# Two small attentions feeding a max-out feed-forward: weights taken in column quarters, batch 0 run along with them, x^T and A^T by transposing DMAs

## The chip, the cores and the metric

The kernel runs on one core of a Trainium2 chip. The metric is device time in microseconds, median of several runs; lower is better. TensorE multiplies matrices and transposes (by a matmul with an identity), VectorE and ScalarE empty its PSUM banks and do elementwise work, GpSimd (POOL) does elementwise work on SBUF, and DMA queues issued from SyncE (SP), ScalarE and POOL move data. Each engine executes its own instructions in program order.

## The reference

B = 8 batches, H = 8 heads, S = 512 rows of x, 32 rows of state, D = 64:

```python
scores = scale * x @ state^T;  a = softmax(scores);  xread = a @ state        # [B,H,512,64]
scores2 = scale * state @ x^T; a2 = softmax(scores2); sread = a2 @ x          # [B,H,32,64]
attn = concat([xread, sread], axis=2)            # heads side by side: [8*544, 512]
out = maximum(attn @ w1, attn @ w2) @ w_out      # w1, w2: 512 x 1024, w_out: 1024 x 512
```

Inputs and output are float32; the kernel multiplies in bfloat16.

## The kernel before, in words

max(x w1, x w2) is computed as x w2 + relu(x (w1 - w2)). So `wcat` holds w1 - w2 (1024 columns) and beside it w2 @ w_out (512 columns), and for every batch the kernel multiplies the state by `wcat` once (`u_sw`, result `SW`, 1536 columns). With A^T, the transposed attention weights (`AT`), a batch's feed-forward (`moe`) is then: L1, 8 tiles of 2 matmuls SW^T A^T, each followed by a relu into `r`; L2, for 4 row blocks 2 matmuls of A^T with SW's last 512 columns and 8 of r with w_out; copy out and store.

The attention of a batch is a list of eight units (`att_units`): `u_xt` twice (8 TensorE transposes of x each and a copy out of PSUM), `u_sc` twice (8 small score matmuls, exp on ScalarE, row sums and reciprocal on VectorE, the normalising multiply on POOL), `u_sr` twice (the state rows' attention; a column of ones in xb gives its sums), `u_at` (8 transposes for A^T and a copy), `u_srt` (4 transposes of the state rows' result). The units of batches 0 to 2 run before the loop; those of batch b + 3 are put between the tiles of batch b's feed-forward, as is `u_sw` of batch b + 1. The order of instructions is the order of the program text.

Ahead of the loop: x of batches 0 to 2 and the states are loaded, then w2 and w1, each as two DMAs to 64 partitions, and w_out with a casting DMA from POOL's queue. `w_t` casts w2 and transposes it on TensorE (32 transposes), `w_wo` multiplies w2 by w_out (32 matmuls of 512 columns), VectorE subtracts w2 from w1, and `u_sw` runs for batch 0. `moe_sread` treats the state rows of all batches in one pass near the end. All PSUM tiles come from one pool of eight banks.

Copies, casts and exits from PSUM go through the helper `copy`, whose lines the profile shows: L58 is ScalarE, L60 VectorE, L62 POOL. L235 is L1, L244 and L246 are L2, L226 and L228 the relus, L147 the x transposes, L189 A^T, L197 the state rows' transposes, L178 `u_sr`, L213 `u_sw`, L161 the scores, L284 and L290 w2's transposes and its product.

Of the kernel before, what the change touches and what calls it, by code (L numbers as in the profile page):

```python
# [8 lines left out]
F32 = mybir.dt.float32  # L9
# [6 lines left out]
def kernel(  # L16
# [9 lines left out]

# [48 lines left out]
    load_x(0)  # L79
    s_f = stage.tile([128, B // 4, DM], F32)  # L80
    for b in range(B):
        nc.scalar.dma_start(
            out=s_f[32 * (b % 4):32 * (b % 4) + 32, b // 4, :].rearrange("n (h d) -> n h d", h=H),
            in_=state[b].rearrange("h n d -> n h d"),
        )
    load_x(1)
    load_x(2)
    w2f = stage.tile([128, 4, FF], F32)
    w1f = stage.tile([128, 4, FF], F32)
    for wf, w in ((w2f, moe_w2), (w1f, moe_w1)):  # L90
# [6 lines left out]
    wo = consts.tile([128, NF, DM], BF16)
    wcat = consts.tile([128, 4, WC], BF16)
    w2b = stage.tile([128, 4, FF], BF16)
    w2t = stage.tile([128, 4, NF, 128], BF16)  # L100


    s_bf = stage.tile([128, B // 4, DM], BF16)
    s_b2 = stage.tile([128, B // 4, 4, 2, D], BF16)
    sbd = consts.tile([128, B, 4, 2 * Ns], BF16)
    nc.vector.memset(sbd, 0.0)
    st2 = consts.tile([128, 4, B * Ns], BF16)

    def states(bb):
        copy("V", s_bf[:, bb, :], s_f[:, bb, :])  # L110
        p = bank(BF16)
        for k in range(4):
            nc.tensor.transpose(p[:, k * 128:(k + 1) * 128], s_bf[:, bb, k * 128:(k + 1) * 128], ident)  # L113
        for jj in range(2):
            copy("A" if jj else "V",
                 sbd[64 * jj:64 * jj + 64, 4 * bb:4 * bb + 4, :, 32 * jj:32 * jj + 32],
                 p[64 * jj:64 * jj + 64, 0:512].rearrange("p (k b n) -> p b k n", k=4, b=4))
        copy("P", s_b2[:, bb], s_f[:, bb, :].rearrange("p (g i d) -> p i g d", g=2, i=4))
        p = bank(BF16)
        for i in range(4):  # L120
            nc.tensor.transpose(p[:, i * 128:(i + 1) * 128], s_b2[:, bb, i].rearrange("p g d -> p (g d)"), ident)
        copy("V", st2[:, :, 128 * bb:128 * bb + 128],
             p[:, 0:512].rearrange("p (i t) -> p i t", i=4))


    sread_t = consts.tile([128, 4, B * Ns], BF16)
    AT, SW = {}, {}
    st = {}

    def cast_x(b, engs=("P", "P")):  # L130
        xb = xio.tile([128, NC, 2, 258], BF16, tag="xb", name="xb")
        nc.gpsimd.memset(xb[:, :, :, 256:257], 1.0)
        for g in range(2):
            copy(engs[g],
                 xb[:, :, g, 0:256].rearrange("p c (i d) -> p i c d", i=4),
                 xf_t[b][:, 4 * g:4 * g + 4, :].rearrange("p i (c d) -> p i c d", c=NC))
        st[b] = dict(xb=xb)

    def u_xt(b, half):
        d = st[b]  # L140
        if half == 0:
            d["xt"] = at.tile([128, NC, 4, 128], BF16, tag="xt", name="xt")
        p = bank(BF16)
        for cc in range(2):
            c = 2 * half + cc
            for k in range(4):
                nc.tensor.transpose(p[:, (cc * 4 + k) * 128:(cc * 4 + k + 1) * 128],  # L147
                                    d["xb"][:, c, k // 2, (k % 2) * 128:(k % 2) * 128 + 128], ident)
        copy("A" if half else "V", d["xt"][:, 2 * half:2 * half + 2].rearrange("p c k t -> p (c k t)"), p)

    def u_sc(b, half):
        d = st[b]
        if half == 0:
            d["e"] = at.tile([128, NC, H, Ns], BF16, tag="e", name="e")
            d["es"] = at.tile([128, NC, H], F32, tag="es", name="es")
            d["er"] = at.tile([128, NC, H], F32, tag="er", name="er")
            d["a"] = at.tile([128, NC, H, Ns], BF16, tag="a", name="a")
        p = bank()
        for cc in range(2):
            for k in range(4):  # L160
                nc.tensor.matmul(p[:, cc * 256 + k * 64:cc * 256 + k * 64 + 64],  # L161
                                 d["xt"][:, 2 * half + cc, k, :], sbd[:, b, k, :],
                                 start=(cc == 0 and k == 0), stop=(cc == 1 and k == 3))
        sl = slice(2 * half, 2 * half + 2)
        nc.scalar.activation(out=d["e"][:, sl].rearrange("p c h n -> p (c h n)"), in_=p, func=ACTF.Exp, scale=scale)  # L165
        nc.vector.tensor_reduce(d["es"][:, sl], d["e"][:, sl], axis=mybir.AxisListType.X, op=ALU.add)  # L166
        nc.vector.reciprocal(d["er"][:, sl], d["es"][:, sl])  # L167
        nc.gpsimd.tensor_mul(d["a"][:, sl], d["e"][:, sl],  # L168
                             d["er"][:, sl].unsqueeze(3).to_broadcast([128, 2, H, Ns]))

    def u_sr(b, g):
        d = st[b]
        if g == 0:
            d["sr"] = at.tile([128, 4, 2, D], BF16, tag="sr", name="sr")
            d["rr"] = at.tile([128, 2], F32, tag="rr", name="rr")
        p = bank()
        for c in range(NC):
            nc.tensor.matmul(p[:, 0:257], d["e"][:, c, 4 * g:4 * g + 4, :].rearrange("p i n -> p (i n)"),  # L178
                             d["xb"][:, c, g, 0:257], start=(c == 0), stop=(c == NC - 1))
        nc.vector.reciprocal(d["rr"][:, g:g + 1], p[:, 256:257])  # L180
        nc.vector.tensor_scalar(d["sr"][:, :, g, :], p[:, 0:256].rearrange("p (i d) -> p i d", i=4), scalar1=d["rr"][:, g:g + 1], scalar2=None, op0=ALU.mult)

    def u_at(b):
        d = st[b]
        AT[b] = keep.tile([128, 2, NC * 128], BF16, tag="at", name="aT")
        p = bank(BF16)
        for g in range(2):
            for c in range(NC):
                nc.tensor.transpose(p[:, (g * NC + c) * 128:(g * NC + c + 1) * 128],  # L189
                                    d["a"][:, c, 4 * g:4 * g + 4, :].rearrange("p i n -> p (i n)"), ident)  # L190
        copy("V", AT[b].rearrange("p g t -> p (g t)"), p)

    def u_srt(b):
# [12 lines left out]

    def u_sw(b, ch):
        if ch == 0:
            SW[b] = big.tile([128, 2, WC], BF16, tag="sw", name="sw")
        pg = [bank(), bank()]  # L210
        for i in range(4):
            for g in range(2):
                nc.tensor.matmul(pg[g][32 * i:32 * i + 32, :],  # L213
                                 st2[64 * g:64 * g + 64, i, b * Ns:(b + 1) * Ns],
                                 wcat[64 * g:64 * g + 64, i, ch * 512:(ch + 1) * 512],
                                 start=True, stop=True)
        for g in range(2):
            copy("A" if g else "V", SW[b][:, g, ch * 512:(ch + 1) * 512], pg[g])

# [10 lines left out]
    def moe(b, fill):  # L230
        r = big.tile([128, NF, NC * 128], BF16, tag="r", name="r")
        for f in range(NF):
# [4 lines left out]
            for u in fill.get(f, ()):  # L237
                u()
# [122 lines left out]
```

The softmax here doesn't subtract the row's maximum and nothing guards it: scores larger than these inputs give would overflow.

## Time and profile before

| | |
|---|---|
| median of 3 runs | 203.4 us (202.53 to 203.79) |
| span of the profiled execution, first to last instruction | 200.5 us |
| TensorE busy | 160.0 us (80%) |
| VectorE, ScalarE, POOL busy | 92.3, 70.6, 34.3 us |
| first L1 matmul of batch 0 | 64.44 us after the span's start |
| moved by DMA | 25.35 MB |

The run times are taken without the profiler; the profiled execution has only its span, and what lies around it (launch and end) is the difference to the medians. TensorE's matmuls are pipelined: one of 512 columns is shown as 379 ns long, while its successor starts 216 ns after it, so durations of groups are read from one start to the next start.

### The profile page before, as it was taken

The numbers are of one execution on the slowest core, as the hardware profiler recorded it, in microseconds if no ns is written. First come the engines' busy times: TensorE is split into PE (matmuls) and PEld (weight loads), VectorE is DVE, ScalarE is ACT, GpSimd is POOL, SyncE is SP. The second block draws the span as 40 slices with busy tenths as digits, with TensorE's granted clock in tenths as the row PEclk, the third lists the DMA queues.
The fourth block names the chain that finished last, engine by engine and source line by source line (L and its number), as shares of the span: only waits on it lengthen the run. The fifth ranks groups of instructions, "written<-read, shape, count | busy, mean of one in ns | idle before, by whom it ended". The sixth has DMA issues, their size and how long they took to land.

```text
span 200.5 us, 2915 instructions
## 1 busy us (share of the span) xinstructions
PE 160.0 (80%) x1192; PEld 83.1 (41%) x1192; DVE 92.3 (46%) x171; ACT 70.6 (35%) x123; POOL 34.3 (17%) x47
## 2 busy tenths in 40 slices
PE   0020364386599989999999999999999999999991
PEld 0010343365344545544644554554454474344440
DVE  1120262136686775484476458448436322632610
ACT  0050143740425812552281182255234230722311
POOL 1010491004340070043016007004000000000000
PEclk9999995566999999999999999999999999999999
DMA  5999999999100000480191075040013042300522
GB/s 179 308 301 227 215 215 219 246 348 309 50 3 0 0 5 0 168 252 3 52 304 65 0 233 190 0 183 29 0 52 157 3 167 67 80 3 0 211 105 105
DMA packets 16557, 25.35 MB, mean 126 GB/s; under 512 B 2848, under 2 KB 14112, under 8 KB 15648
## 3 DMA queue, kind: packets, MB, share of 16 engines
q1 hardware_dynamic: 13328, 23.60, 38.7%
q0 software_dynamic: 1040, 1.05, 3.1%
q10 hardware_dynamic: 2176, 0.52, 1.3%
q8 instruction: 9, 0.15, 0.3%
q14 instruction: 4, 0.03, 0.0%
HBM read 17.30 MB, written 8.91 MB: 131 GB/s over the span
## 4 chain that ended last, share of the span: by engine, by line
PE 61%; DMA 10%; DVE 9%; ACT 9%; POOL 6%; issue 3%; ACTq 1%; DVEq 0%; POOLq 0%
PE ps L246 24%; DMA s_f<-in_state_dram 10%; PE ps L235 9%; PE ps L244 6%; DVE es L166 4%; PE ps L290 3%; PE ps L147 3%; DVE r L228 3%; PE ps L213 3%; POOL a L168 3%; PE ps L178 2%; PE ps L189 2%; ACT e L165 2%; PE ps L284 2%; ACT xt L58 2%
## 5 line engine op out<-in xcount | busy, mean ns | idle before, releaser
L246 PE MATMUL ps<-wo,r 128*128 128x512 bf16 x256 | 61.3, 379 | 1.4 <-DVE r L228 1.4
L246 PEld LDWEIGHTS <-r 128*128 128x128 bf16 x256 | 25.0, 98 | 33.5 <-DVE r L228 3.9
L235 PE MATMUL ps<-aT,sw 128*128 128x512 bf16 x128 | 33.4, 380 | 0.1
L58 ACT COPY ob<-ps 128x512 f32<-128x512 f32 x16 | 9.4, 586 | 67.5 <-PE ps L246 67.5
L168 POOL TENSOR_TENSOR a<-e,er 128x512 bf16<-128x512 bf16 x16 | 16.6, 1048 | 85.1 <-DVE er L167 71.6
L228 DVE TENSOR_SCALAR r<-ps 128x512 bf16<-128x512 f32 x32 | 21.4, 670 | 11.0 <-PE ps L235 10.9
L226 ACT ACTIVATE r<-ps 128x512 bf16<-128x512 f32 x32 | 19.4, 607 | 4.8 <-PE ps L235 4.8
L244 PE MATMUL ps<-sw,aT 128*128 128x512 bf16 x64 | 19.2, 381 | 0.0
L60 DVE COPY ob<-ps 128x512 f32<-128x512 f32 x16 | 11.0, 688 | 17.5 <-PE ps L246 16.1
L113 PE MATMUL ps<-ident,s_bf 128*128 128x128 bf16 x8 | 1.2, 306 | 22.0 <-DVE s_bf L60 22.0
L60 DVE CAST sw<-ps 128x512 bf16<-128x512 f32 x24 | 16.2, 680 | 5.2 <-PE ps L213 5.2
L166 DVE TENSOR_REDUCE es<-e 128x16 f32<-128x512 bf16 x16 | 10.7, 670 | 9.2 <-ACT e L165 9.2
L58 ACT CAST sw<-ps 128x512 bf16<-128x512 f32 x24 | 13.9, 591 | 2.2 <-PE ps L213 2.2
L235 PEld LDWEIGHTS <-sw 128*128 128x128 bf16 x128 | 10.5, 98 | 9.3 <-issue 1.6
L62 POOL CAST xb<-xf 128x1024 bf16<-128x1024 f32 x14 | 14.2, 1042 | 0.0
L147 PE MATMUL ps<-ident,xb 128*128 128x128 bf16 x128 | 11.7, 252 | 0.0
L147 PEld LDWEIGHTS <-xb 128*128 128x128 bf16 x128 | 10.5, 117 | 2.4
L60 DVE COPY xt<-ps 128x1024 bf16<-128x1024 bf16 x8 | 5.5, 692 | 10.9 <-PE ps L147 10.9
L178 PE MATMUL ps<-xb,e 128*128 128x257 bf16 x64 | 9.7, 274 | 0.9 <-ACT e L165 0.6
L58 ACT COPY xt<-ps 128x1024 bf16<-128x1024 bf16 x8 | 8.1, 1009 | 5.3 <-PE ps L147 4.0
L113 PEld LDWEIGHTS <-s_bf 128*128 128x128 bf16 x8 | 0.7, 130 | 22.3 <-DVE s_bf L60 22.3
L165 ACT ACTIVATE e<-ps 128x512 bf16<-128x512 f32 x16 | 9.8, 612 | 0.0
(53 smaller groups left out, 140.6 us busy)
## 6 DMA issues: line engine op xcount, KB each, us to landing
xf<-in_x_dram SPq DMA_DIRECT2D x20, 512.0 KB, 7.3
out_dram<-ob SPq DMA_DIRECT2D x7, 1024.0 KB, 4.3
w2f<-in_moe_w_dram SPq DMA_DIRECT2D x2, 1024.0 KB, 12.3
w1f<-in_moe_w_dram SPq DMA_DIRECT2D x2, 1024.0 KB, 20.3
wo<-in_moe_w_out_dram POOLq DMA_DIRECT2D x1, 1024.0 KB, 18.2
out_dram<-ob SPq DMA_DIRECT2D x2, 512.0 KB, 2.6
s_f<-in_state_dram ACTq DMA_DIRECT2D x8, 64.0 KB, 6.9
out_dram<-obs SPq DMA_DIRECT2D x8, 64.0 KB, 1.7
```

The lines of the kernel that those rows point to most:

```text
L58: nc.scalar.copy(o, i)
L60: nc.vector.tensor_copy(o, i)
L62: nc.gpsimd.tensor_copy(o, i)
L147: nc.tensor.transpose(p[:, (cc * 4 + k) * 128:(cc * 4 + k + 1) * 128], d["xb"][:, c, k // 2, (k % 2) * 128:(k % 2) * 128 + 128], ident)
L165: nc.scalar.activation(out=d["e"][:, sl].rearrange("p c h n -> p (c h n)"), in_=p, func=ACTF.Exp, scale=scale)
L166: nc.vector.tensor_reduce(d["es"][:, sl], d["e"][:, sl], axis=mybir.AxisListType.X, op=ALU.add)
L168: nc.gpsimd.tensor_mul(d["a"][:, sl], d["e"][:, sl], d["er"][:, sl].unsqueeze(3).to_broadcast([128, 2, H, Ns]))
L226: nc.scalar.activation(out=o, in_=p, func=ACTF.Relu)
L228: nc.vector.tensor_scalar(o, p, scalar1=0.0, scalar2=None, op0=ALU.max)
L235: nc.tensor.matmul(p, SW[b][:, g, f * 128:(f + 1) * 128], AT[b][:, g, :], start=(g == 0), stop=(g == 1))
L244: nc.tensor.matmul(p, AT[b][:, g, cs], SW[b][:, g, FF:WC], start=(g == 0), stop=False)
L246: nc.tensor.matmul(p, r[:, f, cs], wo[:, f, :], start=False, stop=(f == NF - 1))
```

## The change

Weights come in four column quarters of 256, each as three DMAs to 128 partitions (w2, w1, w_out in float32, cast on an engine). State loads take 2 KB rows, those of batch 0 first. Batch 0's attention, L1 and L2 are cut to fit the quarters: each quarter is cast, transposed, subtracted and multiplied by the state (`sw`), then two L1 tiles and their share of L2 run, L2 accumulating in four PSUM banks over all quarters (`l2_part`, `l2_open`). w2 @ w_out is done in two halves (`w_wo`). Batch 1's attention lies in between, with TensorE transposes. From batch 2 on, x^T and A^T are written by transposing DMAs on SP's queue (`xt_dma`, `at_dma`), and a batch's attention runs within the batch before it: scores and normalisation after its L1, `sw` and `sread_mm` between its L2 blocks. `sread_mm` uses outputs of 64 partitions and a column of ones apart. PSUM is split in two pools of four banks: `ps`, and `pa` for L2 and the earliest work. At the start some matmuls on zeros run (`idle`). Cut to its core:

```diff
-    for wf, w in ((w2f, moe_w2), (w1f, moe_w1)):
-        for g in range(2):
-            nc.sync.dma_start(
-                out=wf[64 * g:64 * g + 64],
-                in_=w[256 * g:256 * g + 256].rearrange("(i d) f -> d i f", i=4),
-            )
+    def load_wq(q):
+        for wf, w, tag in ((w2f, moe_w2, "w2f"), (w1f, moe_w1, "w1f")):
+            wf[q] = stage.tile([128, 4, FQ], F32, tag=tag, bufs=3, name=tag)
+            nc.sync.dma_start(out=wf[q], in_=w[:, q * FQ:(q + 1) * FQ].rearrange("(i p) f -> p i f", p=128))
+        wof[q] = stage.tile([128, 2, DM], F32, tag="wof", bufs=3, name="wof")
+        nc.sync.dma_start(out=wof[q], in_=moe_w_out[q * FQ:(q + 1) * FQ, :].rearrange("(f p) n -> p f n", p=128))
...
+    def xt_dma(b):
+        d = st[b]
+        d["xt"] = at.tile([128, NC, 4, 128], BF16, tag="xt", name="xt")
+        nc.sync.dma_start_transpose(out=d["xt"].rearrange("p c k t -> p (c k) t"),
+                                    in_=d["xb"].rearrange("p c m -> p (c m)"))
...
+    def at_dma(b):
+        d = st[b]
+        AT[b] = keep.tile([128, 2, NC, 128], BF16, tag="at", name="aT")
+        nc.sync.dma_start_transpose(out=AT[b].rearrange("p g c t -> p (g c) t"),
+                                    in_=d["a"].rearrange("p g c i n -> p (g c i n)"))
...
+    def sread_mm(b, pool=None):
+        d = st[b]
+        p = bank(F32, pool)
+        d["srp"] = p
+        for c in range(NC):
+            xv = d["xb"][:, c].rearrange("p (i g d) -> p g i d", g=2, d=D)
+            for g in range(2):
+                for ih in range(2):
+                    nc.tensor.matmul(p[64 * ih:64 * ih + 64, g * 128:(g + 1) * 128],
+                                     d["e"][:, g, c, 2 * ih:2 * ih + 2].rearrange("p i n -> p (i n)"),
+                                     xv[:, g, 2 * ih:2 * ih + 2],
+                                     start=(c == 0 and g == 0), stop=(c == NC - 1 and g == 1), skip_group_check=True)
+        for g in range(2):
+            for c in range(NC):
+                nc.tensor.matmul(p[:, 256 + g:257 + g], d["e"][:, g, c].rearrange("p i n -> p (i n)"), ones[:, 0:1],
+                                 start=False, stop=(c == NC - 1), skip_group_check=True)
...
+    def l2_part(q, first):
+        for c in range(NC):
+            if first:
+                ACC[c] = bank(F32, pa)
+            l2_f(0, c, ACC[c], (2 * q, 2 * q + 1), first, False)
...
+    load_states(sf0, 0, 1)
+    load_x(0)
+    for q in range(3):
+        load_wq(q)
+    load_states(sfr, 1, B)
+    load_x(1)
+    load_wq(3)
+    load_x(2)
+    load_x(3)
...
+    idle(7)
+    states(sf0, sb0, 0, 1, "V", "A", "V", pa)
+    cast_x(0, ("V", "V"))
+    xt_pe(0, 0, "A", pa)
+    xt_pe(0, 1, "V", pa)
+    w2_cast(0, "P")
+    scores(0, 0)
+    w2_tr(0, "A")
+    norm(0, 0, "V")
+    scores(0, 1)
+    w_sub(0, 2, 4, "P")
+    norm(0, 1, "V")
+    w_sub(0, 0, 2, "V")
+    at_pe(0, ("A", "V"), pa)
+    wo_cast(0, "P")
+    sw(0, 0, FQ)
+    sread_mm(0, pa)
+    w2_cast(1, "A")
+    l1(0, 0)
+    l1(0, 1)
...
+    w_sub(1, 0, 2, "V")
+    w_sub(1, 2, 4, "P")
+    wo_cast(1, "P")
+    w2_tr(1, "V")
+    sw(0, FQ, 2 * FQ)
+    l2_part(0, True)
+    l1(0, 2)
+    l1(0, 3)
+    w2_cast(2, "A")
+    for i in range(4):
+        w_wo(0, i)
...
+    sread_tr(0, "A")
+    l2_part(1, False)
+    w2_tr(2, "V")
+    sw(0, 2 * FQ, 3 * FQ)
+    states(sfr, sbr, 1, B, "P", "A", "V")
+    cast_x(1, ("V", "A"))
+    l1(0, 4)
+    l1(0, 5)
+    xt_pe(1, 0, "A")
+    xt_pe(1, 1, "V")
+    w2_cast(3, "A")
+    l2_part(2, False)
+    scores(1, 0)
+    scores(1, 1)
+    w_sub(3, 0, 2, "V")
+    w_sub(3, 2, 4, "P")
+    norm(1, 0, "P")
+    norm(1, 1, "P")
+    wo_cast(3, "A")
+    w2_tr(3, "V")
+    sw(0, 3 * FQ, 4 * FQ)
+    l1(0, 6)
+    l1(0, 7)
+    cast_x(2, ("P", "P"))
+    xt_dma(2)
+    sread_mm(1)
+    for i in range(4):
+        w_wo(1, i)
+    sread_norm(1)
+    at_pe(1, ("A", "V"))
+    l2_part(3, False)
+    sw(1, 0, 512)
+    sw(0, FF, WC)
+    sw(1, 512, 1024)
+    for c in range(NC):
+        l2_open(0, c, ACC[c], False, True)
+        l2_out(0, c, ACC[c], "A" if c % 2 else "V")
...
+    for b in range(1, B):
+        n = b + 1
+        if b + 2 < B:
+            cast_x(b + 2, ("P", "P"))
+            xt_dma(b + 2)
         for f in range(NF):
...
+            l1(b, f)
         if n < B:
...
+            for hh in range(2):
+                scores(n, hh)
+            for hh in range(2):
+                norm(n, hh, "P")
+            at_dma(n)
+            if b + 3 < B:
+                load_x(b + 3)
+        else:
             moe_sread()
+        for c in range(NC):
+            l2(b, c)
+            if n < B:
+                if c < 3:
+                    sw(n, 512 * c, 512 * c + 512)
+                if c == 1:
+                    sread_mm(n)
+                if c == 2:
+                    sread_norm(n)
+                if c == 3:
+                    sread_tr(n, "A")
...
+        if n < B:
+            store(b)
```

## Rows read from the trace of the kernel before

**Rows 1.** The page's first two parts: busy time; clock in 40 slices.
```profile
PE 160.0 (80%) x1192; PEld 83.1 (41%) x1192; DVE 92.3 (46%) x171; ACT 70.6 (35%) x123; POOL 34.3 (17%) x47
...
PEclk9999995566999999999999999999999999999999
```

**Rows 2.** Table by stage: stretch, length, busy per engine, clock, DMA share, GB/s.
```profile
23.10:56.20 33.10, 20.50 (x197) 15.60 (x198) 14.11 (x34) 13.24 (x18) 12.28 (x16) 0.74 0.90 224
...
107.58:124.29 16.71, 16.50 (x133) 8.30 (x132) 9.72 (x20) 6.98 (x13) 4.10 (x6) 1.00 0.40 127
...
162.03:170.71 8.68, 8.68 (x58) 5.44 (x56) 2.39 (x5) 2.02 (x5) 0.00 (x0) 1.00 0.36 138
...
184.13:196.22 12.09, 12.09 (x57) 5.26 (x54) 4.15 (x6) 3.46 (x6) 0.00 (x0) 1.00 0.32 131
196.22:200.50 4.28, 0.00 (x0) 0.00 (x0) 0.00 (x0) 0.59 (x1) 0.00 (x0) 1.00 0.30 123
```

**Rows 3.** Chain of waits, first 64 us: start, length, what ended the wait.
```profile
2.35 7.67 DMA s_f<-in_state_dram
10.04 12.45 DMA s_f<-in_state_dram
...
36.34 1.99 PE ps L284 x16
...
56.36 6.91 PE ps L290 x32
```

**Rows 4.** Timeline of TensorE, 23.5 to 27 us: start, length, instructions.
```profile
23.98 1.91 PE L147 MATMUL ps<-ident,xb 128*128 128x128 bf16 x16
```

**Rows 5.** Chain of waits, 105 to 125 us: TensorE's groups in a steady batch.
```profile
109.30 0.44 PE ps L178 x4
109.74 0.34 PE ps L213 x8
...
113.22 1.73 PE ps L246 x8
114.95 0.22 PE ps L197 x4
...
115.61 0.45 PE ps L147 x8
```

**Rows 6.** Table by stage of three loading stretches; the last column is GB/s.
```profile
24.00:29.00 5.00, 4.07 (x42) 2.97 (x40) 2.77 (x6) 2.69 (x4) 5.00 (x8) 1.00 1.03 218
40.00:45.00 5.00, 3.97 (x42) 3.33 (x42) 1.69 (x3) 2.17 (x4) 0.00 (x0) 0.64 1.11 347
42.00:45.00 3.00, 2.35 (x29) 1.70 (x26) 1.13 (x3) 1.85 (x3) 0.00 (x0) 0.74 1.10 371
```

**Rows 7.** Timeline of TensorE, 117.9 to 120 us.
```profile
118.51 0.40 PE L161 MATMUL ps<-sbd,xt 128*128 128x64 bf16 x8
118.74 1.03 PE L235 MATMUL ps<-aT,sw 128*128 128x512 bf16 x4
```

**Rows 8.** Groups of instructions by form: busy us, mean ns of one, idle before.
```profile
L168 POOL TENSOR_TENSOR a<-e,er 128x512 bf16<-128x512 bf16 x16 | 16.6, 1048 | 85.1 <-DVE er L167 71.6 <-ACT sw L58 13.4
...
L58 ACT COPY xt<-ps 128x1024 bf16<-128x1024 bf16 x8 | 8.1, 1009 | 5.3 <-PE ps L147 4.0 <-DVE xt L60 1.3
...
L60 DVE COPY aT<-ps 128x1024 bf16<-128x1024 bf16 x8 | 5.5, 684 | 3.1 <-PE ps L189 3.1
L311 DVE TENSOR_TENSOR wcat<-w1f,w2f 128x1024 bf16<-128x1024 f32 x4 | 5.3, 1376 | 0.0
```

**Rows 9.** DMA queues and issues of the page: packets, MB, share; KB, us to landing.
```profile
q10 hardware_dynamic: 2176, 0.52, 1.3%
...
out_dram<-ob SPq DMA_DIRECT2D x7, 1024.0 KB, 4.3
...
out_dram<-obs SPq DMA_DIRECT2D x8, 64.0 KB, 1.7
```

**Rows 10.** Line 74, the x loads: from issue to landing.
```profile
DMA to landing us min/median/max: 4.3/7.3/28.3
```

More of the change, by code (lines that the diff above doesn't have):

```diff
@@ L97 @@
[L97 to L123, printed above, removed]
@@ L151, in u_sc @@
-    def u_sc(b, half):
-        d = st[b]
[L153 to L169, printed above, removed]
@@ new lines, with l1, l2_open @@
+    R, OB, ACC = {}, {}, [None] * NC
+    def l1(b, f, eng=None):
+        if f == 0:
+            R[b] = big.tile([128, NF, NC * 128], BF16, tag="r", name="r")
+        p = bank()
+        for g in range(2):
+            nc.tensor.matmul(p, SW[b][:, g, f * 128:(f + 1) * 128], AT[b][:, g].rearrange("p c t -> p (c t)"),
+                             start=(g == 0), stop=(g == 1))
+        relu(R[b][:, f, :], p, eng)
+    def l2_open(b, c, p, start, stop):
+        for g in range(2):
+            nc.tensor.matmul(p, AT[b][:, g, c, :], SW[b][:, g, FF:WC], start=(start and g == 0), stop=(stop and g == 1))
@@ new lines, in l2_f, with l2_out, l2 @@
+    def l2_f(b, c, p, fs, start, stop):
+        for j, f in enumerate(fs):
+            nc.tensor.matmul(p, R[b][:, f, c * 128:(c + 1) * 128], wo[:, f, :],
+                             start=(start and j == 0), stop=(stop and j == len(fs) - 1))
+    def l2_out(b, c, p, eng):
+        if c == 0:
+            OB[b] = big.tile([128, NC, DM], F32, tag="ob", name="ob")
+        copy(eng, OB[b][:, c, :], p)
+    def l2(b, c):
+        p = bank(F32, pa)
+        l2_open(b, c, p, True, False)
+        l2_f(b, c, p, range(NF), False, True)
+        l2_out(b, c, p, "A" if c % 2 else "V")
@@ L277, in moe_sread @@
                 nc.sync.dma_start(out=out[b * L + S:(b + 1) * L], in_=ob[32 * q:32 * q + 32, t, :])
-    def w_t(i):
-        copy("A", w2b[:, i, :], w2f[:, i, :])
-        p = bank(BF16)
-        for f in range(NF):
-            nc.tensor.transpose(p[:, f * 128:(f + 1) * 128], w2b[:, i, f * 128:(f + 1) * 128], ident)
-        copy("V" if i % 2 else "A", w2t[:, i].rearrange("p f t -> p (f t)"), p)
-    def w_wo(i):
-        p = bank()
-        for f in range(NF):
-            nc.tensor.matmul(p, w2t[:, i, f, :], wo[:, f, :], start=(f == 0), stop=(f == NF - 1))
-        copy("A", wcat[:, i, FF:WC], p)
@@ new lines, in w2_tr, with w_sub @@
+    def w2_tr(q, eng, pool=None):
+        p = bank(BF16, pool)
+        for f in range(2):
+            for i in range(4):
+                nc.tensor.transpose(p[:, (f * 4 + i) * 128:(f * 4 + i + 1) * 128],
+                                    w2b[q][:, i, f * 128:(f + 1) * 128], ident)
+        copy(eng, w2t[:, 2 * q:2 * q + 2].rearrange("p f i t -> p (f i t)"), p)
+    def w_sub(q, i0, i1, eng):
+        (nc.gpsimd if eng == "P" else nc.vector).tensor_sub(
+            wd[:, i0:i1, q * FQ:(q + 1) * FQ], w1f[q][:, i0:i1], w2f[q][:, i0:i1])
@@ new lines, in wo_cast, with w_wo, idle @@
+    def wo_cast(q, eng):
+        copy(eng, wo[:, 2 * q:2 * q + 2, :], wof[q])
+    def w_wo(half, i):
+        p = bank()
+        for j in range(4):
+            f = 4 * half + j
+            nc.tensor.matmul(p, w2t[:, f, i, :], wo[:, f, :], start=(j == 0), stop=(j == 3))
+        if half == 0:
+            copy("A" if i % 2 else "V", w2acc[:, i, :], p)
+        else:
+            nc.vector.tensor_tensor(wwo[:, i, :], p, w2acc[:, i, :], op=ALU.add)
+    def idle(n):
+        p = bank(F32, pa)
+        for j in range(n):
+            nc.tensor.matmul(p, wz[:, 0:128], wz, start=True, stop=True)
```

276 lines of the change are left out of this document (141 added, 135 removed).

## The prediction

> **What bounds the kernel now.** I read the page's first two parts first: TensorE is busy 80% of the span, no other engine half of it, so the 40 us in which TensorE does nothing and the work it need not do are what can be won [rows 1]. The table by stage says where they lie [rows 2]. A steady batch (107.58 to 124.29) takes 16.71 us, with TensorE busy for 16.50: this stage is bound by TensorE's own instruction count. The last batch is 12.09 us of pure L1 and L2, the state rows' own pass (`moe_sread`) 8.68 us, and 4.28 us follow the last matmul (copy, store, end). Before the loop it is different: `moe(0)` starts at 64.44, and between 23.1 and 56.2 TensorE is busy 20.5 of 33.1 us at a mean clock of 0.74, with DMA busy for 0.90 of the time. The chain of waits of that stretch [rows 3] shows why: the second half of the states lands only at 22.5; then, since engines work in program order, ScalarE's weight casts, TensorE's transposes and the copies take turns; and the 32 matmuls of `w_wo` (6.91 us) stand alone after all weights are in. Nothing of a MoE batch is done by then. Also the clock: the page's PEclk line shows 9 in the first slices [rows 1], but 16 transposes take 1.91 us there [rows 4], against 0.45 us for 8 later [rows 5], so TensorE stood on its lower level (1.2 GHz), with the record merely silent.
>
> **The start: loads.** Weights were loaded as two halves of 64 partitions, in 4 KB rows; the stretch that holds only those moves 218 GB/s, while a stretch with x alone (128 partitions, 1 KB rows) moves 371 [rows 6]. The quarters have the x shape, 1 KB or 2 KB rows on 128 partitions; I take 347, the 40 to 45 us figure over a mixed stretch [rows 6], with 218 as the other end. Up to the last quarter lie 64 KB and 0.46 MB of states, two x of 1.05 MB and four quarters of 1.57 MB: 8.9 MB, 25.7 us, from the first DMA at 2.35 [rows 3] to 28 us; at 218 GB/s it would be 43. The states now come in 2 KB rows, the first batch's alone and first, so the wait to 22.5 goes.
>
> **The start: TensorE's work.** What is issued before batch 1, at the full clock: 32 (`w_wo`), 16 (L1) and 40 (L2) matmuls of 512 columns, 88 by 0.216 us (1.73 for 8 [rows 5]) = 19.0; 84 transposes (w2 32, xt 32, at 16, sread 4) by 0.056 = 4.7, states 0.7; scores 2 by 0.46 (8 in 0.23 by the next start [rows 7]); four full `sw` by 0.34 and four quarter ones by some 0.25 (2.4); `sread_mm` 2 by 1.1 (below): 31 us. I walked the program order with the landings above (a weight tensor's 0.52 MB every 1.6 us, x0 whole at 6.6, quarter 0 at 8.2, 9.8, 11.4). Batch 0's chain: cast, transposes, ScalarE copy 1.01, exp, reduce, reciprocal, multiply (2 us together), then the subtraction queued behind it on VectorE (1.376 for 1024, so 0.7), transposes, `sw` and its copies, `sread_mm` [rows 8]: first L1 at 15.5 us. Of the 31 us, 27 come after that. Waits on the walk: 1.5 where `sw` of quarter 1 waits for its subtraction, 0.8 and 0.5 around quarter 2 (VectorE and ScalarE have the states' and x1's copies ahead of `sw`'s), 2.2 where `sw` of quarter 3 waits behind the two reduces of batch 1: some 4.5. That gives 47; 2 us more for matmuls at the lower level, since up to 15 us TensorE is mostly idle and then runs its first bursts slow, as the trace of before shows for sparse stretches. **Batch 1 starts at 49**, between 44 (no waits) and 60 (weights at 218 GB/s: 43 plus 12 us of TensorE work behind the last quarter and its handovers). `idle(7)` lies in time in which nothing has landed, and costs nothing.
>
> **A steady batch.** Removed from TensorE: 16 x^T transposes (2 by 0.45), 8 A^T (as many as one half of x^T, 0.45), 2 of 4 in `sread_tr` (0.11): 1.46 us [rows 5]. With them go the xt and aT copies from VectorE and ScalarE (0.68 twice and 1.01 [rows 8]), neither of which bounds, and perhaps part of the 0.66 us that the steady batch has above its instruction sum (16.06: L1 3.46, L2 8.64, xt 0.90, at 0.45, srt 0.22, sr 0.88, sw 1.03, scores 0.46). `sread_mm` replaces 8 matmuls of 257 columns (0.88) by 16 of 128 columns on half the array's columns and 8 of one column. No row has that form: the floor is 0.66 (half of 0.88 if two halves run side by side, and 8 by 0.028, the small score matmuls), the ceiling 16 by 0.056 plus 8 by 0.056 = 1.34; I take 1.1, the old 0.88 plus 0.22, since that is nearest in columns streamed. Sum 3.46 + 8.64 + 0.46 + 1.03 + 0.11 + 1.1 = 14.8, plus half of the 0.66: **15.1 us**, bounds 14.4 and 15.7. VectorE and ScalarE carry under 10 us of it, POOL two multiplies of 1.05 [rows 8] and two casts. L1 now runs without other work between its tiles: two tiles take TensorE 0.86 us, and their two evictions run side by side on two engines, each shorter than that, which fits in four banks.
>
> **The transposing DMAs.** They move to SP's queue: per batch `xt_dma` (512 KB), `at_dma` (256 KB), two x loads, one store, in that order, one behind the other. Before `xt_dma(b+2)` stands `store(b-1)`, issued 0.7 us after the batch begins, landing 4.3 us later: 5.0 [rows 9]. `at_dma(b+1)` waits for POOL's second multiply: scores at 3.5 to 3.9, exp to 5.6, reduces and reciprocals to 7, multiplies (1.05 each) to 8.3. Behind that wait stand only the loads of x(b+3), not needed for a batch. The next L1 needs A^T at 15.1. The trace of before has no such transfer. Its nearest row is the states' 256-byte packets: 2176 in 1.3% of 16 engines' span, 19 ns each [rows 9], so 2048 of them on 16 engines 2.4 us for x^T, 1.2 us for A^T, plus some 1.7 us to land (the 64 KB stores). Let k be how many times slower than this a transposed byte is: A^T lands at max(8.3, 5.0 + 2.4k) + 1.2k + 1.7. At k = 1 that is 11.2, hidden; to k = 2.3 nothing shows; beyond, each k costs 3.6 us in each of six batches. The near end is k = 0.6 (the 371 GB/s stretch), the far end some 12 (the longest x landing, 28.3 us for the same bytes [rows 10]); I take 1 to 2, by the packet row, as the far one was mostly queueing.
>
> Two rules of the Trainium skill bear on this and disagree. "VectorE: DVE Perf Modes", section "The three transpose paths", gives 1309 ns for a 128 by 128 block by DMA and 390 ns by TensorE, and advises TensorE. By it, if blocks didn't overlap (an estimate), k would be 8.7 and the total some 300 us. "Advanced Engine Details and Errata", "X-Bar Transpose (TRN2)", calls such DMAs as fast as regular ones, by which they would stay hidden. Against its 390 ns the trace has 56 ns per transpose in a warm batch [rows 5]. Whether the DMA figure holds in a batch of 16 blocks no run here shows yet.
>
> **The sum.** 49 + 6 by 15.1 (batches 1 to 6) + 12.09 + 8.68 (batch 7 with `moe_sread`) + 4.28 = 164.7 us of span against 200.5. The median of the three runs, 203.4, is 2.9 above the profiled span; with that added, 167.6: **168 us**.
>
> **Rivals.** A: the transposing DMAs show, k from 2.3 to 4: `L1` then waits for A^T each batch. k = 3 gives 17.5 against 15.1, six times, 182 us. For it: no margin but 4 us at k = 1, and 1 MB stores and loads on the same engines. Against: DMA is busy for 0.40 of a steady batch now.
> B: slower than before. The same wait at k above 4: 36 us of gain over six batches is 5.9 us each, so A^T at 21.1 is break-even, k = 4.0. At k = 6, 28.3 us per batch, 79 us more: 247 us. For it: the crossing from 128 partitions to 128 others is nothing the packet row shows. Against: needs under 15% of what plain loads reach.
> The 1309 ns of the Trainium skill ("VectorE: DVE Perf Modes", "The three transpose paths") would come out in this form.
> C: the start doesn't shorten: quarters load at 218 GB/s or the clock stays low; batch 1 at 60, 179 us.
>
> **How the numbers follow.** Forecast 0.70, A 0.13, B 0.12, C 0.05. The forecast's own range is 159 (44 and 14.4) to 177. Range of all: below 159 some 0.04, B and the worst of A (k over 3.5) above 190: 159 to 190 leaves out 0.18. About 1% is what a measurement of this kernel can tell from no change (the three runs span 0.6%). Faster: forecast, C and nearly all A, 0.86; within 1%, 0.02; slower 0.12.
>
> **What would show it.** In the profile after: batch 1's first L1 near 49; DMA above 300 GB/s until 28 us; steady batches of 15.1 us with L1 never waiting for a DMA on aT; transposing DMAs landing under 7 us from issue. Wrong if L1 waits on aT in each batch (k), if `sw` in the first 50 us waits for landings rather than for VectorE, or if `sread_mm` takes over 1.4 us.

## The result: 172.0 us, a ratio of 0.8515, and the profile after

| | before | after |
|---|---|---|
| median of 4 runs, taken in turns | 202.97 us | 171.97 us (171.11 to 172.71) |
| ratio, 95% interval | | 0.8515 [0.844, 0.859] |
| span of the profiled execution; its own time | 200.5 us | 170.9 us; 172.71 us |
| first L1 matmul of batch 1 (`moe(1)`) | 81.58 us | 56.71 us |

The forecast was 168 us in a range of 159 to 190, so direction and range held and the time came out 4 us above the figure. The page's first two parts of the kernel after, to be read against [rows 1]:

```profile
PE 147.9 (87%) x1164; PEld 73.7 (43%) x1183; DVE 89.7 (52%) x163; ACT 66.6 (39%) x127; POOL 38.0 (22%) x41
...
PEclk9999999987999999999999999999999999999999
```

TensorE's busy time fell by 12 us and the span by 30: more than half of the gain is idle time, not work. Up to batch 1's first L1 it is 24.9 us, behind it 4.7; the cut is not even, since the kernel before had the attention of batches 1 to 3 behind it at that point and the changed one that of batch 1 alone. The table by stage (stretch, length, busy of PE, PEld, DVE, ACT, POOL, clock, DMA share, GB/s) says where it went; it answers to [rows 2]:

```profile
0.00:30.00 30.00, 17.69 (x138) 10.45 (x140) 15.13 (x26) 9.76 (x15) 10.07 (x14) 1.00 0.99 314
30.00:56.71 26.71, 21.38 (x199) 11.46 (x202) 17.33 (x29) 11.65 (x21) 7.26 (x7) 0.94 0.30 81
...
101.35:116.12 14.77, 14.64 (x123) 6.81 (x123) 8.31 (x16) 6.44 (x13) 4.06 (x4) 1.00 0.71 196
145.66:170.90 25.24, 20.82 (x113) 10.84 (x112) 6.54 (x11) 6.40 (x14) 0.00 (x0) 0.99 0.30 105
```

The first two rows are the start, the third a steady batch, still TensorE end to end (14.64 of 14.77; the difference is matmuls whose records are missing, see below), the fourth what follows the loop's sixth batch. Set beside the forecast's terms: start 56.71 against 49 (+7.7); six batches 88.95, or 14.83 each, against 15.1 (-1.6); the rest 25.24 against 25.05 (+0.2); and 1.07 instead of 2.9 between span and median (-1.8). 167.6 + 7.7 - 1.6 + 0.2 - 1.8 = 172.1. So one term was wrong by much, the start, and the others took back some 3 us, which is luck. The last of them shows it: each of the four runs is 1.8 us above its own span, so both 2.9 and 1.07 depend on which execution was profiled.

The steady batch in TensorE's timeline (start, length, instructions, idle before), the counterpart of [rows 5]:

```profile
101.35 3.62 PE L264 MATMUL ps<-aT,sw 128*128 128x512 bf16 x16
104.80 0.63 PE L162 MATMUL ps<-sbd,xt 128*128 128x64 bf16 x16
105.49 0.38 PE L270 MATMUL acc<-sw,aT 128*128 128x512 bf16 x1
...
110.46 0.64 PE L203 MATMUL ps<-xb,e 128*64 128x128 bf16 x16
111.03 0.35 PE L209 MATMUL ps<-ones,e 128*128 128x1 bf16 x8
111.46 0.38 PE L270 MATMUL acc<-sw,aT 128*128 128x512 bf16 x1
...
116.12 1.24 PE L264 MATMUL ps<-aT,sw 128*128 128x512 bf16 x5
```

L1 takes 3.45 (start to start), and no row has a bracket: nothing waits. After the scores and after `sread_mm` one of the two L270 matmuls has no record here (x1, where there are two), so their lengths can't be read from these rows. Of `e2_pe_transposes` (below), which has the same two groups, the records are whole:

```profile
77.11 0.63 PE L162 MATMUL ps<-sbd,xt 128*128 128x64 bf16 x16
77.57 0.60 PE L270 MATMUL acc<-sw,aT 128*128 128x512 bf16 x2
...
82.77 0.64 PE L203 MATMUL ps<-xb,e 128*64 128x128 bf16 x16
83.34 0.35 PE L209 MATMUL ps<-ones,e 128*128 128x1 bf16 x8
83.55 0.59 PE L270 MATMUL acc<-sw,aT 128*128 128x512 bf16 x2
```

The scores take 0.46 us and `sread_mm` 0.78 (forecast 1.1 between 0.66 and 1.34). `e1_state_first`, whose steady batch has the change's instructions, 14.77 us and whole records too, has 0.47 and 0.79, and TensorE busy for 14.77 of 14.77. SP's timeline of the change's batch shows the transposing DMAs, with the time for which each issue held SP's queue:

```profile
102.05 0.36 SPq L290 DMA_DIRECT2D out_dram<-ob  x1
102.52 4.71 SPq L135 DMA_TRANSPOSE xt<-xb  x1
109.19 1.23 SPq L182 DMA_TRANSPOSE aT<-a  x1
110.47 1.15 SPq L87 DMA_DIRECT2D xf<-in_x_dram  x2
```

And the list of DMA issues (count, KB, median us from issue to landing):

```profile
out_dram<-ob SPq DMA_DIRECT2D x7, 1024.0 KB, 5.7
...
xt<-xb SPq DMA_TRANSPOSE x6, 7.7
aT<-a SPq DMA_TRANSPOSE x6, 3.0
```

A^T is issued 7.8 us into the batch and lands 3.0 later, 3.9 us before the L1 that needs it at 116.12. In the summed waits of TensorE not one waits for a DMA.

The start is another matter. TensorE's waits (waiter, awaited, us in total, times, longest):

```profile
PE acc L117 <- DVE sb L60: 4.2, 1, 4.2
PE acc L191 <- DVE a L174: 3.3, 1, 3.3
PE ps L264 <- DVE sw L60: 2.8, 2, 2.4
PE acc L146 <- DVE xb L60: 1.8, 2, 1.4
PE ps L241 <- DVE wd L328: 1.7, 2, 1.2
PE ps L146 <- DVE xb L60: 1.4, 1, 1.4
```

All six largest name VectorE. What held VectorE back first is in the chain of waits (start, length, what ended the wait):

```profile
0.73 1.27 ACTq L105
...
2.03 5.64 DMA sf<-in_state_dram
...
7.77 0.69 DVE sb L60
...
9.53 2.15 DVE xb L60 x2
```

Batch 0's states, 64 KB issued from ScalarE's queue beside x, land 5.64 us after their issue. Their cast is the first thing that VectorE does with a load, so the casts of x stand behind it in program order and begin at 9.53.

### The profile page after: what moved, and what is told of

The parts are those of the page before. It is cut to its first block, busy times and chain, and to the rows that moved or that the text cites. A ratio compares the mean times of both kernels' runs of the same rounds, so it can differ in the third digit from the quotient of the medians.

```text
span 170.9 us, 2878 instructions
## 1 busy us (share of the span) xinstructions
PE 147.9 (87%) x1164; PEld 73.7 (43%) x1183; DVE 89.7 (52%) x163; ACT 66.6 (39%) x127; POOL 38.0 (22%) x41
## 4 chain that ended last, share of the span: by engine, by line
PE 80%; DVE 8%; ACT 4%; DMA 3%; issue 2%; ACTq 1%; DVEq 0%
PE acc L274 33%; PE ps L264 16%; PE acc L270 9%; PE ps L241 4%; PE ps L338 4%; DMA sf<-in_state_dram 3%; PE ps L203 2%; PE ps L298 2%; PE ps L162 2%; PE acc L308 2%; DVE xb L60 2%; DVE wd L328 1%; PE ps L209 1%; DVE es L172 1%; PE acc L306 1%
## 5 line engine op out<-in xcount | busy, mean ns | idle before, releaser
L274 PE MATMUL acc<-wo,r 128*128 128x512 bf16 x252 | 60.7, 383 | 0.4 <-ACT xt L58 0.2
L58 ACT CAST sw<-ps 128x512 bf16<-128x512 f32 (+1 forms) x26 | 14.3, 555 | 33.3 <-PE ps L241 23.0
L60 DVE CAST sw<-ps 128x512 bf16<-128x512 f32 (+1 forms) x26 | 16.5, 643 | 11.1 <-PE ps L241 11.0
L60 DVE COPY ob<-acc 128x512 f32<-128x512 f32 x16 | 10.8, 672 | 21.8 <-PE acc L274 21.6
L58 ACT COPY ob<-acc 128x512 f32<-128x512 f32 x16 | 9.4, 585 | 27.7 <-PE acc L274 26.8
L264 PEld LDWEIGHTS <-sw 128*128 128x128 bf16 x128 | 12.1, 99 | 16.5 <-DVE sw L60 3.1
L270 PE MATMUL acc<-sw,aT 128*128 128x512 bf16 x52 | 16.2, 381 | 1.0 <-DVE sw L60 0.2
L241 PE MATMUL ps<-wd,sbd 64*32 64x512 bf16 (+1 forms) x144 | 7.2, 369 | 2.2 <-DVE wd L328 1.7
L241 PEld LDWEIGHTS <-sbd 64*32 64x32 bf16 x208 | 3.3, 89 | 11.6 <-issue 11.3
L338 PE MATMUL ps<-wo,w2t 128*128 128x512 bf16 x31 | 7.0, 379 | 0.1
L270 PEld LDWEIGHTS <-aT 128*128 128x128 bf16 x64 | 4.4, 97 | 4.8 <-issue 3.1
L162 PEld LDWEIGHTS <-xt 128*128 128x128 bf16 x128 | 5.4, 103 | 1.7
L162 PE MATMUL ps<-sbd,xt 128*128 128x64 bf16 x128 | 5.7, 200 | 0.0
```

The costliest lines, as they stand in the source:

```text
L58: nc.scalar.copy(o, i)
L60: nc.vector.tensor_copy(o, i)
L162: nc.tensor.matmul(pv[:, c, kk], d["xt"][:, c, k, :], sbd[:, b, k, :], start=(c == 0 and kk == 0), stop=(c == NC - 1 and kk == 1))
L241: nc.tensor.matmul(pg[g][32 * i:32 * i + 32, 0:n], sbd[64 * g:64 * g + 64, b, i, 32 * g:32 * g + 32], rhs, start=True, stop=True)
L264: nc.tensor.matmul(p, SW[b][:, g, f * 128:(f + 1) * 128], AT[b][:, g].rearrange("p c t -> p (c t)"), start=(g == 0), stop=(g == 1))
L270: nc.tensor.matmul(p, AT[b][:, g, c, :], SW[b][:, g, FF:WC], start=(start and g == 0), stop=(stop and g == 1))
```

## The experiments

Each kernel is the changed one with the edit shown; for the last two, which join earlier edits, only the new part is shown. Times are medians; the kernel before was timed on the same chip in each set (201.8, 204.4 and 202.9 us).

**The states first on SP's queue** (`e1_state_first`), against the theory that the start's shortfall is the state load.

```diff
-                nc.scalar.dma_start(out=t[:, j, :], in_=s[:, :, j, :])
+                nc.sync.dma_start(out=t[:, j, :], in_=s[:, :, j, :])
```

> The states of batch 0 are issued on SP's queue ahead of x instead of on ScalarE's queue beside it. In the changed kernel their cast on VectorE starts at 7.77 us, and the casts of x of batch 0, next in VectorE's order, at 9.53. Theory (the late states hold batch 0's chain): the cast starts near 4 us, x^T by 8, but the second half of the scores stands behind the transposes of weight quarter 0 in TensorE's order, whose landing (10.0) and cast (1.1) don't move; so first L1 comes 1.5 to 2.5 us earlier than 20.77 and the total falls by as much, to 169.5 to 170.5. Rival (the start is bound by the later quarters or by later waits): first L1 earlier, the total within 0.5 us of 172.

171.72 us, ratio 0.8547 [0.8484, 0.8611]: the same as the change. But the trace moved where it should: the states' cast began at 3.98 (7.77 before), x's first cast at 5.84 (9.53), the first L1 at 17.64 (20.77; 21.85 in another execution of the change, `e0_after` below). By batch 1 only 1.3 us of those 3.1 were left (55.41). Two rows of TensorE's timeline, first of this kernel, then of the changed one, show where the rest went:

```profile
22.04 3.58 PE L274 MATMUL acc<-wo,r 128*128 128x512 bf16 x8
```

```profile
24.98 1.90 PE L274 MATMUL acc<-wo,r 128*128 128x512 bf16 x8
```

The same eight matmuls took 3.58 us here and 1.90 there: this run was still on the lower clock level when the change's run had left it (granted clock 0.51 against 1.00). `e0_after` shows the change itself on the lower level in these matmuls, so this run does not show that the earlier start brought it about.

**x^T and A^T on TensorE again** (`e2_pe_transposes`): the steady batch without its transposing DMAs, the rest of the change kept.

```diff
-    xt_dma(2)
...
-            xt_dma(b + 2)
...
+            if n < B and f == 3:
+                xt_pe(n, 0, "A")
+            if n < B and f == 5:
+                xt_pe(n, 1, "V")
...
-            at_dma(n)
...
+                    at_pe(n, ("A", "V"))
```

> x^T and A^T of batches 2 to 7 are made on TensorE again (x^T after L1 tiles 3 and 5, A^T after the third L2 block); all else as in the changed kernel. Theory (the transposing DMAs are hidden, and what they give is TensorE's time alone): a steady batch of 14.77 + 24 transposes by 0.056 = 16.1 us, six of them 8.1 us more, 180 us. Rival 1 (the DMAs cost something elsewhere, by queue or bandwidth): under 4 us more. Rival 2 (TensorE has slack): no change.

184.63 us, 0.9206 [0.9108, 0.9303]: 12.7 us of the 31 belong to the transposing DMAs. A steady batch takes 16.70 us (72.74 to 89.44) against 14.77, six times 1.93 or 11.6 us more. The kernel before had 16.71, so without the transposing DMAs nothing of the steady batch's gain is left. TensorE's timeline of it:

```profile
74.47 0.61 PE L146 MATMUL ps<-ident,xb 128*128 128x128 bf16 x8
74.92 1.03 PE L264 MATMUL ps<-aT,sw 128*128 128x512 bf16 x4
...
86.95 0.38 PE L191 MATMUL ps<-ident,a 128*128 128x128 bf16 x4 [0.40 <-ACT sw L58]
```

24 transposes at 0.45 for 8 are 1.35 us, and the bracket adds a wait of 0.40: A^T's bank comes free only when ScalarE has copied `sw` out of it. Some 0.2 us stay unassigned. A transpose on TensorE thus costs its instructions here and a turn in the PSUM pool.

**Weights by 64 partitions** (`e3_w64`), the price of rival C alone:

```diff
-            nc.sync.dma_start(out=wf[q], in_=w[:, q * FQ:(q + 1) * FQ].rearrange("(i p) f -> p i f", p=128))
+            for h in range(2):
+                nc.sync.dma_start(out=wf[q][64 * h:64 * h + 64],
+                                  in_=w[:, q * FQ:(q + 1) * FQ].rearrange("(i p) f -> p i f", p=128)[64 * h:64 * h + 64])
```

> Each quarter of w1 and w2 is loaded as two DMAs to 64 partitions, the form of the kernel before. Theory of the prediction (loads of quarters set the start): 4.2 MB at 218 instead of 350 GB/s are 7 us later at the last quarter, total up by 7 to 11 us, 179 to 183. Rival that the trace after suggests (from quarter 1 on the program order of VectorE, ScalarE and TensorE sets the start; the loads are ahead by 3 to 9 us): up by 0 to 2 us.

174.0 us, 0.8655 [0.8588, 0.8722]; batch 1 at 57.88. The stretch of 10 to 30 us, of the change and then of this kernel:

```profile
10.00:30.00 20.00, 14.15 (x123) 9.28 (x125) 12.49 (x21) 8.02 (x12) 9.37 (x8) 1.00 1.08 338
```

```profile
10.00:30.00 20.00, 14.07 (x123) 9.08 (x124) 11.74 (x22) 7.79 (x12) 6.66 (x6) 0.64 1.11 211
```

The load rate fell from 338 to 211 GB/s, near the forecast's two figures, 347 and 218 [rows 6], with the DMA engines as busy. The rows are 1 KB in both kernels, so the lower rate goes with the 64 partitions and not with the 4 KB rows of the kernel before. Yet batch 1 moved by 1.2 us only, less than the 2.6 us by which two executions of the change differ (`e0_after`): the last quarter is not what the start waits for. The forecast's bound of 60 us for this case was not far off, but for another reason.

**One and two transposing DMAs more per batch** (`e4_one_more`, `e4_two_more`): x^T of the next batch is written again ahead of A^T, once or twice, each after the one before (redundant work; the output is the same). They measure the cover that hides the DMAs.

```diff
+            for j in range(1):   # 2 in the second kernel
+                nc.sync.dma_start_transpose(out=st[n]["xt"].rearrange("p c k t -> p (c k) t"),
+                                            in_=st[n]["xb"].rearrange("p c m -> p (c m)"))
             at_dma(n)
```

> One more 512 KB transposing DMA per batch, of x into the spent x^T tile, on SP's queue right ahead of the one for A^T: batches 2 to 7. Theory (A^T lands 3.9 us before L1 needs it, and 512 KB of such packets take 2.5 to 3 us): no change, within 1 us of 172. Rival (transposing DMAs follow each other slowly, as their 7.7 us from issue to landing in the list of issues reads): 7.7 minus 3.9, 4 us in each of six batches, 195 us.

> Two more 512 KB transposing DMAs per batch ahead of the one for A^T, the second into the same tile, so that it waits for the first to land. With one more nothing changed. Theory (a slack of 3.9 us, eaten by 2 to 3 us per transfer and some 2 us for the wait): A^T now lands 1 to 5 us late in each of six batches, total 178 to 200. Rival (the slack is larger than the trace reads, or the queue works off more than it seems): within 1 us of 172.

One more: 173.64 us, 0.8635 [0.8574, 0.8697], and its steady batch is still 14.77 us, with DMA busy for 0.99 of it:

```profile
72.74:87.51 14.77, 14.77 (x125) 6.83 (x123) 8.30 (x16) 6.44 (x13) 3.21 (x4) 1.00 0.99 216
```

Two more: 190.92 us (187.59 to 191.89). Now L1 waits, in five of the six batches. TensorE's waits and timeline of that kernel:

```profile
PE ps L264 <- DMA aT<-a: 12.1, 5, 4.2
```

```profile
75.30 3.63 PE L264 MATMUL ps<-aT,sw 128*128 128x512 bf16 x16 [1.42 <-DMA aT<-a]
...
93.42 5.31 PE L264 MATMUL ps<-aT,sw 128*128 128x512 bf16 x16 [3.18 <-DMA aT<-a]
```

That is rival A's form, reached only with twice 512 KB added. The waits (12.1 us) do not make up the 18.2 us that the span grew. After the wait of 3.18 us, and after another of 4.16, L1 took 5.31 instead of 3.63, on the lower clock level for part of it (granted clock 0.67 and 0.68), which adds 3.4. Another 1.9 us lie ahead of batch 1 (58.61 against 56.71), where this edit does nothing, and 0.8 stay unassigned. After the three waits of 1.42 to 1.80 us L1 took 3.63 as before. So the transfer that began to show was paid for twice in two of the five batches.

**The change again** (`e0_after`), as the control of the second set:

> The changed kernel once more, beside the next three on one chip: 171 to 173 us by every theory.

173.77 us (172.73 to 175.24), 1.8 above its first median. Its profiled execution has batch 1 at 59.28, where the first had 56.71; 1.1 us of the difference lie ahead of the first L1 (21.85 against 20.77). TensorE's table by stage shows most of the rest (the clock is the third figure from the end):

```profile
26.16:29.46 3.30, 3.30 (x16) 1.19 (x9) 0.55 (x2) 0.37 (x1) 0.00 (x0) 0.51 1.08 363
```

The first share of L2, 1.73 us at the full clock, took 3.30 at a granted clock of 0.51. The change's start varies by this much from one execution to another.

**Three single edits of the start's order**: batch 1's normalisation behind the last L1 tiles (`e5_norm_late`), both of batch 1's x casts on POOL (`e6_x1_pool`), filler matmuls ahead of A^T's transposes (`e9_warm`).

```diff
-    norm(1, 0, "P")
-    norm(1, 1, "P")
...
     l1(0, 7)
+    norm(1, 0, "P")
+    norm(1, 1, "P")
```

```diff
-    cast_x(1, ("V", "A"))
+    cast_x(1, ("P", "P"))
```

```diff
+    idle(7)
     at_pe(0, ("A", "V"), pa)
```

> The normalisation of batch 1 (two reduces on VectorE, two multiplies on POOL) is issued after the last two L1 tiles of batch 0 instead of before the last quarter's transposes and product. In the changed kernel TensorE waits 2.42 us at 42.7 to 45.1 for VectorE's copy of that product, which stands behind the reduces. Theory (program order of the engines sets the start from quarter 1 on): the wait falls under 0.8 us, total down by 1.5 to 2, at 170. Rival (the time comes back, at the later waits on VectorE or where A^T of batch 1 is needed): within 0.5 us of the control.

> x of batch 1 is cast on POOL alone instead of on VectorE and ScalarE, where the casts stand between copies that TensorE waits for. POOL is idle from 26 to 30.7 us. Theory (program order): of the 1.42 us wait before batch 1's transposes and the late relus some 1.5 us go, 170.5. Rival (x of batch 1 lands too late for that, or the next wait takes it): within 0.5 us.

> Seven more matmuls on zeros ahead of batch 0's A^T transposes, in a stretch (14.5 to 17.8 us) in which TensorE waits. With the states loaded earlier the first L1 came 3.1 us sooner, but the first share of L2 then ran at the lower clock (3.4 us instead of 1.7). Theory (the clock, not only order, costs time in the first 25 us): the work from 17.8 to 24.7 runs at the higher level, first L1 and all after it 1 to 2.5 us earlier, 169.5 to 171. Rival (those stretches wait for VectorE and the landings anyway): within 0.5 us, or 0.3 later for the matmuls themselves.

172.68 (170.83 to 174.67), 172.47 (171.35 to 173.22) and 172.17 us (170.47 to 173.18): each about 1 to 1.6 us below the control, with ranges that overlap, so by time none is decided. The waits did what was asked. With the first, TensorE's 2.42 us for the fourth `sw` became 0.81; this is its timeline:

```profile
43.85 0.39 PE L264 MATMUL ps<-aT,sw 128*128 128x512 bf16 x1 [0.81 <-DVE sw L60]
```

With the second the wait of 1.42 us for the cast of x1 is gone. The third shortened the stretch from A^T's transposes to the first L1 from 3.01 us to 1.61. Batch 1 began at 55.79, 56.84 and 57.18, where the change had 56.71 and 59.28, so by the start as a whole none is decided either.

**Without the matmuls on zeros** (`e8_no_idle`):

```diff
-    idle(7)
```

> The seven matmuls on zeros at the very start are left out (TensorE's first work is then the states' transposes). Prediction's step: they cost nothing and give nothing, since the clock has fallen again before weights arrive; within 0.8 us of the control, which itself runs from 171 to 175. Rival (they lift the clock for the transposes of x): 1 us slower.

171.93 us, 0.8456 [0.8407, 0.8506], the same as the change. The seven matmuls lie where nothing has landed and cost nothing, as the forecast said; nor do they keep the clock up until the real work begins: the first 8 transposes of x took 1.03 us with them and 1.04 without.

**The start's mends together, without and with filler matmuls** (`combo`, `combo_warm`): states first, the second half of batch 0's scores ahead of w2's transposes, the late normalisation and x1's casts on POOL; the second kernel has matmuls on zeros besides, at three places where TensorE would wait.

```diff
+    scores(0, 1)
+    idle(3)            # combo_warm alone
     w2_tr(0, "A")
...
-    scores(0, 1)
...
+    idle(6)            # combo_warm alone
     at_pe(0, ("A", "V"), pa)
...
+    idle(4)            # combo_warm alone
     sw(0, FQ, 2 * FQ)
```

> The states of batch 0 first on SP's queue, both score halves of batch 0 ahead of the first weight quarter's transposes, batch 1's normalisation late, x of batch 1 cast on POOL. By the runs before: 3.1 us earlier at the first L1 plus 0.5 for the scores, 1.6 and 1.1 at the two waits; if the clock does not take it back, 5 to 6 us, 167; with the first quarters at the lower clock, 169 to 170. Rival (later waits take it all): 172.

> The kernel before it, with 3, 6 and 4 more matmuls on zeros where TensorE waits in the first 22 us (ahead of the first quarter's transposes, of A^T of batch 0, and of the second quarter's product). Theory (the clock of the start is the remaining term: it adds 1 to 4 us and differs from run to run): 1.5 to 3 us faster than without them, 164.5 to 167, and a narrower spread. Rival (matmuls on zeros cost what they give): the same within 0.7 us.

167.48 us, 0.8286 [0.8239, 0.8332], for the first, its six runs from 164.9 to 169.49; 164.42 us, 0.8102 [0.8069, 0.8135], for the second, 163.58 to 164.82. The fillers add 13 matmuls and take 3 us off the median, and the spread falls from 4.6 us to 1.2. TensorE's timeline of the second, from A^T's transposes on (L347 is the filler):

```profile
13.49 2.17 PE L347 MATMUL acc<-wz 128*128 128x512 bf16 x6
15.50 0.61 PE L191 MATMUL acc<-ident,a 128*128 128x128 bf16 x8
...
17.05 1.02 PE L264 MATMUL ps<-aT,sw 128*128 128x512 bf16 x3
...
48.15 0.59 PE L264 MATMUL ps<-aT,sw 128*128 128x512 bf16 x2
```

From A^T's transposes to L1 it is 1.55 us here and 3.01 in the change, of which these are the rows:

```profile
17.76 1.04 PE L191 MATMUL acc<-ident,a 128*128 128x128 bf16 x8 [3.29 <-DVE a L174]
...
20.77 0.59 PE L264 MATMUL ps<-aT,sw 128*128 128x512 bf16 x1
```

Batch 1 begins at 48.15, where the forecast had the change at 49. This kernel beats both others, the change by 7.5 us. But the profile of `combo` is of its fastest execution (164.9 us), and without any filler it is almost as short:

```profile
48.56 0.59 PE L264 MATMUL ps<-aT,sw 128*128 128x512 bf16 x2
```

That stretch takes 3.01 us there too, yet its first L1 stands at 16.63, ahead of the 17.05 here. So the two profiles do not show where the 3 us between the medians lie.

## Why the prediction was right, and where its sum was off

**The steady batch.** Right in mechanism: TensorE's instruction count bounds it, and taking 24 of its transposes away shortens it. The size, 14.77 us against 15.1, is in part luck, since three terms were off and nearly cancel: by the whole records of `e1_state_first`, `sread_mm` took 0.79 instead of 1.1, near the floor of 0.66, L2 took 8.93 instead of 8.64, and of the 0.66 us left over the instruction sum, of which I kept half, nothing is left. Putting the transposes back gave 1.93 us per batch, of which instructions are 1.35.

**The transposing DMAs.** Right: hidden, with k near the 1 of the packet row. The 512 KB of x^T issued at 47.57, with no store ahead of it, held SP's queue for 1.91 us, and its bytes moved at 213 GB/s with the DMA engines busy throughout (table by stage, share and GB/s last):

```profile
49.50:51.30 1.80, 1.80 (x16) 1.09 (x15) 1.46 (x4) 0.53 (x1) 0.01 (x1) 1.00 1.15 213
```

At that rate 512 KB take 2.5 us, where k = 1 gives 2.4; A^T lands 3.0 us after its issue, where k = 1 gives 2.9. The margin of 3.9 us (forecast: some 4) took one further 512 KB and not two. Rivals A and B fall with this. One of the signs failed: behind a store x^T lands 7.6 to 8.2 us after its issue, not under 7. That sign left the store out; by the prediction's own 5.0 + 2.4 + 1.7 it is 9.1 us into the batch, 7.9 after an issue at 1.2.

By the Trainium skill's "Advanced Engine Details and Errata", "X-Bar Transpose (TRN2)", such DMAs are as fast as regular ones. The trace agrees with that for the states' 256-byte packets, the row that k is measured by, and not for the weights' quarters, which moved at 338 GB/s. By the 1309 ns per block of the Trainium skill's "VectorE: DVE Perf Modes", "The three transpose paths", the 8 blocks of A^T would take 10.5 us one after the other, an estimate that the 3.0 us contradict.

**The start: the mis-sized term.** The step that failed is "the states now come in 2 KB rows, the first batch's alone and first, so the wait to 22.5 goes". The wait to 22.5 did go, but these states were neither alone nor first, though the change was described so: they came from ScalarE's queue beside x on SP's and landed at 7.67, and their cast stands ahead of those of x in VectorE's program order. I walked the landings of x and of the weights and gave the states none. The first L1 came 5.3 us late (20.77 against 15.5); moving the states gave back 3.1 of it. Another 1.5 lie between A^T's transposes and L1 (3.01 us against 1.55): 1.1 of the lower clock, and a wait of 0.40 for a subtraction on VectorE. Some 0.7 stay unassigned.

From the first L1 to batch 1 it took 35.94 us instead of 33.5 (27 of work, 4.5 of waits, 2 of clock). Waits came to 6.4: the two foreseen of `sw` behind the reduces (2.42) and behind the subtraction (1.25), 1.42 for x1's cast, which I had not listed, and smaller ones. The remaining 29.5 us are work, at times at the lower level: the stretch from 37.06 to 41.35, 16 transposes and 8 matmuls, took 4.29 us in the change's profile and 2.63 in that of `e3_w64`. In `combo_warm` that part is 31.1 us with 3.4 of waits and 1 of fillers (four of 512 columns, 1.03), which leaves 26.7: the 27 us of TensorE's work were right, though the terms listed for the whole start add up to 29.9 us and not to the 31 that they were taken from. So the shortfall is program order on VectorE (shown by the waits that the edits removed, and by `combo` in time) and a clock for which 2 us were allowed, and which took 1.1 ahead of the first L1 and some 2.5 behind it (29.5 less 27). Together: 3.1 for the states, 0.4 and 1.9 for waits, 1.6 for the clock and the 0.7 unassigned are the 7.7 us. A possible cause of some of VectorE's delays shows in rows of its timeline, the same subtraction of 512 columns at 17.62 and at 39.50:

```profile
17.62 1.52 DVE L328 TENSOR_TENSOR wd<-w1f,w2f 128x512 bf16<-128x512 f32 x1
...
39.50 0.68 DVE L328 TENSOR_TENSOR wd<-w1f,w2f 128x512 bf16<-128x512 f32 x1
```

Beside the first, POOL casts w_out:

```profile
17.24 1.36 POOL L62 CAST wo<-wof 128x1024 bf16<-128x1024 f32 x1
```

Beside the second POOL does nothing. Another, at 30.98, took 1.56 us beside a subtraction of POOL's (30.72 to 31.99). The Trainium skill, "SBUF — State Buffer", "Who interferes with whom", has it that an instruction of VectorE with two inputs in SBUF and one of GpSimd that reads SBUF shut each other out; these rows agree with that, and no run here varied it by itself.

**Rival C** came nearest of the rivals (batch 1 at 60, 179 us; nearer to the 56.71 than the forecast's 49), with the load as its reason. Loads were at 338 GB/s, and slowing them to 211 moved batch 1 by less than two executions of the change differ. Its other half, the clock, was part of what happened.

**What stays open.** Why one execution of the same kernel leaves the lower level at 24.7 us and another only at 29.5 is not settled. That filler matmuls shorten the median and narrow the spread of `combo` is shown by time; which of the three places does it, and that it is by the clock, is not, since no slower execution of `combo` was traced. No run undoes the interleaving of batch 0 with the loads by itself: that it gave most of the 24.9 us ahead of batch 1 is read from the traces.

## What to carry to other kernels

Where TensorE's own instructions bound a stage and the DMA engines have time to spare, transposes between SBUF tiles can go to transposing DMAs, if their result is needed some microseconds after the issue; measure the cover by adding a transfer, since an uncovered one cost the wait here and, after the two longest waits, the clock as well. In a start, list the landing of every load that an engine's first instructions name, small ones above all: in program order a late 64 KB holds back what lies ready behind it. An early gain can be lost again while TensorE is on its lower level, so follow the gain to the end of the stage before you count it.

## What the runs showed of the hardware that was not expected

- The record of the granted clock is silent until its first change: the change's page shows 9 up to slice 8, while 8 transposes took 1.03 us at 10.29 and 0.61 at 50.34.
- Each of the five transposing DMAs of x^T issued behind a 1 MB store held SP's queue for 4.6 to 6.0 us, against 1.9 for the one with no store ahead. Alone it moved 213 GB/s with the DMA engines busy (1.15).
- Sixteen matmuls of 128 columns with outputs of 64 partitions (`sread_mm`) took 0.57 us, 36 ns each, where a transpose of 128 columns takes 56.
- Reading the same bytes into 64 partitions at a time instead of 128 lowers the rate from 338 to 211 GB/s at an equal busy share of the DMA engines (1.11 and 1.08).
- After waits of 3.18 and 4.16 us in the middle of dense work TensorE ran its next 16 matmuls in 5.31 us instead of 3.63; after waits of 1.42 to 1.80 us it did not slow down. The wait's length alone does not settle it: in the start, the four L1 matmuls after a wait of 2.42 us took 0.97 us in the change's first profile, and those after one of 2.41 us took 1.65 in `e0_after`.
